# One search's order, homes, banks and engines for a two-branch kernel, replaced by another's

## The chip, the cores and the metric

The kernel runs on one core of a Trainium2 chip. The metric is the device time of one execution in microseconds; the median of three runs of the kernel before is 277.72 us (277.55 to 278.22).

## The reference

Two independent branches are computed over 2048 positions and set side by side in a bf16 output of 896 columns.

```python
# branch A: linear attention, 16 heads of 28, x is 2048 x 448
q, k, v = heads of (x @ wqkv)
phi(t) = concat[softmax(t @ w_phi), softmax(-(t @ w_phi))]     # per head, 56 features
kv = phi(k)^T @ v;  z = sum over positions of phi(k)
a = ((phi(q) @ kv) / (phi(q) @ z + 1e-6)) @ wo                   # 2048 x 448

# branch B: state-space convolution, 448 channels, 256 complex states
dt = exp(log_dt);  A = A_re + 1j*A_im
K[d, l] = Re sum_n C[d,n] * exp(dt*A*l)[d,n] * dt*B[d,n]         # l = 0..2047
y = causal convolution of u with K (rfft, product, irfft) + u * Dskip
out = concat([a, y], axis=-1)                                    # 2048 x 896
```

## The kernel before

Every instruction group is first recorded and only then issued. Helpers (`tt`, `act`, `copy`, `mms`, `dma`, `turn`, `total`) add 1366 units to a `Plan`; a unit is one instruction, or one group of matmuls into one PSUM tile. `Plan.run` then walks a string, `ORDER`, whose tokens are a unit's number and a letter for the engine that issues it: P for TensorE (PE), A for ScalarE (ACT), D for VectorE (DVE), G for GpSimd (POOL), S for SyncE (SP). Each engine executes its own units in the order of the string. A letter can be chosen where a helper allows it: `copy` (L342, an eviction from PSUM) is a cast on ACT or on DVE; `total` (L379 or L381, a sum in place) is a DVE add or an accumulating DMA that POOL issues; `dma` (L366) is issued by SP, POOL or ACT.

All of SBUF is one tile of 212,800 bytes a partition. `HOMES` gives each buffer its byte address, and buffers whose lives do not overlap share bytes. `BANKS` gives each PSUM tile one of eight banks. So a unit waits for its operands and for the readers of whatever lay in its home or bank before.

Branch A has sixteen key tiles (`key_tile`: exponentials on ACT, reciprocals L801 and products on DVE, sums over positions on PE), then four query groups (`query`, q0 to q3): exponentials, reciprocals L844 and L847, evictions, a product, a sum, a transpose by DMA (`turn`, L371, SP), the product with `wo`, an eviction and a store.

Branch B transforms u (`signal_spectrum`) and builds K in eight chunks of 56 channels, k = 0 to 7. Each chunk runs through the same cycle:

- `dampings` and `rotations` (rot k): PE makes phases, and ACT applies Exp and Sin to them. Exp and Sin need different tables, so ACT loads a table at each turn (L332 ACT_TABLE_LOAD, 17 in all, before and after).
- `damp` (damp k): POOL sets one row (L731, zero k); DVE multiplies tables `W[k]` and `E[k]` with L322. It needs rot k.
- `hi_tables` (hi k): products on DVE and five sums by `total`, each feeding the next.
- `build_k` (build k.1, then build k.0): 112 matmuls each, both reading `W[k]`; an eviction of each, 128x343.

All eight `W[k]` lie over each other, so rot k+1 on ACT must wait until build k on PE has read `W[k]`. In groups of two chunks follow 36 small DMAs that scatter K into place (`scatter_k`, sc0 to sc3; SP and POOL share them), `kernel_spectrum` (ks), the products `conv_group` (conv g.0 and g.1, DVE, with sums by `total`) and `inverse` (inv, matmuls, evictions, stores).

A part of the early chain of powers of H (`powers`) also uses `total`: units 90, 93, 96 and 99 on POOL, whose result DVE needs for the next doubling.

Of the kernel before, what the change touches and what calls it, by code (L numbers as in the profile page):

```python
# [91 lines left out]
0S 2A 3A 4S 5S 7S 28G 43P 44A 45D 42D 6S 46P 52A 49A 47P 30G 53D 71P 54A 72A 55D 73P 38G 51A 74A 50A 8S 140G 75P 77D  # L92
37S 48A 80D 76P 79D 17S 78D 57A 82D 56A 58D 81D 59D 649P 654A 61A 25S 657A 60A 655A 646P 648A 656A 39S 62D 650A 139G
141S 40S 69A 64A 142G 651A 143D 63D 144D 653A 95D 652A 88D 94D 89D 189S 190G 639P 19S 636P 65A 22S 41G 68A 191D 151P
647A 168P 640A 21S 18S 642A 638A 20S 118P 119A 225P 645A 226A 145P 637A 70D 169A 112P 192D 104D 210P 66D 23S 644A 24S
126P 643A 127A 641A 216P 211A 186P 102A 676D 113A 96G 180P 90G 219P 67D 92D 187A 217A 207P 114P 146A 218G 91D 97D 115A
93G 100A 122P 123A 213P 159P 98D 152A 214A 208A 103D 107A 680D 12S 124P 156P 116P 199P 234P 117A 200A 125A 34G 120P
675D 101D 235A 682D 677D 181A 121A 10S 9S 678D 681D 248P 105A 270P 272A 109D 259P 99G 660D 273A 262A 659D 171P 679D
201P 13S 220A 221G 250A 202A 195P 236G 196A 661D 174P 11S 170S 108D 261A 110A 172A 175A 106D 147P 212G 292P 294A 157A
303P 160A 295A 158G 183P 184A 658S 663D 662D 281P 283A 111D 237P 240A 14S 711D 148A 710D 712G 35G 203S 29G 165P 306A  # L100
664D 284A 166A 209G 239A 305A 149P 251A 204P 336P 150A 338A 153P 193P 188S 205A 194A 690P 154A 339A 665D 215G 666D
667D 669D 668D 670D 672D 671D 176S 696A 709S 714D 197P 687P 691A 155S 700P 673D 713D 688A 715D 27S 716D 693A 717D 198A
718D 297S 674G 685P 683P 689A 692A 695A 719D 694A 720D 708A 701A 707A 731D 721D 26S 1S 703A 161G 697P 698A 727D 699A
31G 725G 705A 173S 704A 314P 83P 722D 228P 206S 723D 684A 84A 129S 724G 686A 177P 702A 726D 229A 178A 179G 706A 85A
325P 730D 222P 733D 231P 223A 728D 833P 298P 842S 317A 227S 729D 732D 87A 264S 736P 328A 844D 843D 1025D 232A 167G
845D 327A 734P 893G 894D 15S 846D 316A 839A 330S 835A 837A 847D 86A 737A 841A 838A 836A 299D 265P 848D 830P 832A 735D
849D 895D 850D 834A 275S 266D 851D 331P 332D 896G 831A 840A 757G 820P 823P 16S 829A 825A 853D 852D 863D 822A 326P 854D
856D 827A 329A 855D 828A 758G 859D 861D 860D 824A 162P 826A 821A 163A 380P 383A 382A 369P 371A 372A 864D 862D 865D
286S 224S 866D 358P 402P 897D 898D 899D 751S 304P 900D 752S 901D 884P 902D 391P 360A 253S 361A 394A 393A 871P 742S
857G 333D 404A 769G 858G 182G 872A 754S 308S 405A 32G 307A 867P 868A 869P 890A 870D 276P 277D 886A 341S 342P 230S 396S  # L110
343D 888A 891A 887A 892A 885A 903D 904D 1026D 889A 770S 363S 164G 881P 874P 385S 905D 765G 883A 882A 1027D 748S 906D
# [5 lines left out]
355D 337P 1018A 1022A 320P 740G 321D 340A 366D 285A 763S 311D 1012P 1013A 260P 322D 1014A 425P 1039G 293P 1020A 1045D
263A 296A 1041D 759S 1017A 1042D 422P 1048D 953S 741S 749S 1021A 1019A 249P 252A 1043D 939S 936S 419P 1044D 421A 427A
951S 1047D 420A 476P 943G 424A 478A 428P 430A 289D 950G 744S 482P 376D 935G 944S 233G 344D 1051P 429A 484A 477A 1049P
929G 750G 760G 1066P 743S 1075S 426A 1052A 483A 423A 1073A 1207D 955S 245D 1063P 1072A 1065A 246P 256D 410D 957G 257P  # L120
267D 247P 258P 269P 947G 1074A 1050A 1070A 268P 279P 377D 300D 280P 291P 302P 290P 301P 312P 1076D 323P 313P 324P
1071A 1064A 335P 334P 345P 356P 773S 346P 357P 1068A 1067A 925S 473P 937S 924S 766S 771G 368P 367P 745S 378P 753G
1056P 1208D 379P 390P 1069A 401P 412P 946S 1077D 1078D 1080D 1061A 1206G 952G 1079D 1081D 1083D 932S 389P 1082D 1053P
400P 411P 949S 474A 1209G 1211D 930S 1084D 475A 1210D 775S 1055A 417D 1085D 416D 1062A 1057A 1054A 755S 780S 1058A
1060A 756S 768S 414D 533P 535A 418D 534A 479P 1086D 413D 931S 415D 1087D 530P 1096D 1088D 138G 954G 928G 772G 767G
431P 1089D 1093D 927G 776P 777A 1059A 785S 786P 455P 456A 439P 440A 443P 1097D 461P 462A 536P 432D 1092D 1212G 790S
778P 444A 481A 433D 480A 781P 782A 779A 783P 130G 787A 457P 459P 1214D 460A 1213D 437P 438A 441P 788P 789A 442A 434D
537A 791P 792A 458A 956S 527P 532A 528A 941G 1099D 1187P 1193A 1190A 945G 435D 1094D 1095D 1098D 793P 794A 531A 529A
137S 784A 1090G 1091G 1100P 1101A 131S 942G 133G 1215G 436D 795D 1102P 922S 1189A 746S 1184P 1197P 1188A 923S 445D
134S 463D 538A 1191A 1103A 1216D 1192A 1185A 1186A 1217D 485P 635S 1200A 1198A 797G 961P 1218G 774D 515P 807D 962A  # L130
1194P 1196A 796D 806D 486D 1205A 1195A 1202A 1199A 799D 1204A 1201A 803P 808D 136S 1128S 487D 965P 446G 539P 1135S
938S 1125S 798D 800P 1105G 1126G 1203A 1222G 516A 963P 1112S 1139G 966A 511P 512A 809G 1259D 488D 1219D 1123S 1257G
1258D 1120S 959S 1220D 1221G 964A 1260G 1223D 1225D 1137G 811G 1134G 489D 1228D 495P 496A 509P 510A 969P 967P 970A
# [52 lines left out]
BANKS = "2246060577464565566424057205213025364344223317722252233000363614704367562041217134315736107506766202\  # L186
# [880 lines left out]
```

## Time and profile before

| What | Value |
|---|---|
| Median of three runs | 277.72 us (277.55 to 278.22) |
| Profiled execution, its own time | 275.77 us |
| Its span, first to last instruction | 274.0 us |
| Mean granted TensorE clock | 0.979 |
| PE, DVE, ACT, POOL busy | 85%, 90%, 86%, 36% of the span |

The profiled execution stands 0.7% under the median of the runs, so changes are added up against 275.77 and then carried over to the median. A busy share is an average over very different stretches. In the lists, a wait is the idle time of an engine just before an instruction, put down to what ended it. In a list of waits the three numbers are the total in us, the number of waits, and the longest one. In a grouped list `x68 | 71.8, 1083 | 4.2` means 68 instructions, 71.8 us busy, 1083 ns each on average, 4.2 us idle ahead of them. Matmuls overlap in the pipeline, so a mean per matmul is longer than their spacing.

### The profile page before, as it was taken

What the parts mean: (1) busy time and instruction counts of PE and PEld (TensorE: products, weight loads), DVE (VectorE), ACT (ScalarE), POOL (GpSimd) and SP (SyncE); (2) the same over time, 40 slices, a digit from 0 to 9 for tenths busy, and PEclk for the clock granted to TensorE, in tenths of its full rate; (3) what the DMA queues carried; (4) which work ended last, traced back from release to release, by engine and by line L of the source; (5) the groups of instructions that cost most, each with busy time, mean ns of one, the idle gap of its engine ahead of it and who ended that gap; (6) DMA issues with size and microseconds to landing.
All of it is one profiled execution on the core that took longest, in us unless ns stands there. A gap on an engine that the chain in (4) does not pass through costs nothing.

```text
span 274.0 us, 10764 instructions
## 1 busy us (share of the span) xinstructions
PE 233.8 (85%) x4620; PEld 199.8 (73%) x4620; DVE 247.1 (90%) x334; ACT 235.0 (86%) x414; POOL 97.3 (36%) x169
## 2 busy tenths in 40 slices
PE   3825788999896797698999998979997998998994
PEld 3724686789786476376669977979895998788964
DVE  1699989999999899799899999997999989999891
ACT  3999999999999998996998999998969992756551
POOL 2400221260113330302942362176757210657450
PEclk9995999999999999999999999998999999999998
DMA  7996996455548797981431699399987797125764
GB/s 188 327 362 119 173 208 118 140 153 129 130 110 126 130 165 115 122 93 22 63 75 19 198 237 203 52 250 164 142 135 105 187 219 138 11 16 93 177 178 113
DMA packets 66969, 39.10 MB, mean 143 GB/s; under 512 B 53372, under 2 KB 62954, under 8 KB 66666
## 3 DMA queue, kind: packets, MB, share of 16 engines
q1 hardware_dynamic: 57914, 23.22, 40.7%
q0 software_dynamic: 8400, 14.94, 28.5%
q8 instruction: 36, 0.59, 1.0%
q10 hardware_dynamic: 608, 0.26, 0.3%
q14 instruction: 11, 0.09, 0.1%
HBM read 13.18 MB, written 6.42 MB: 72 GB/s over the span
## 4 chain that ended last, share of the span: by engine, by line
PE 31%; ACT 30%; DVE 19%; issue 8%; DMA 6%; SPq 4%; POOL 0%; ACTq 0%; DVEq 0%; POOLq 0%
PE psum L351 31%; ACT sbuf L332 20%; DVE sbuf L322 16%; ACT sbuf L342 5%; DMA sbuf<-sbuf 4%; SPq L366 4%; ACT L332 4%; ACT sbuf L337 1%; DVE sbuf L379 1%; DMA sbuf<-in_B_A_re_dram 1%; DVE sbuf L326 1%; DVE sbuf L545 0%; POOL sbuf L381 0%; DVE sbuf L342 0%; DVE sbuf L801 0%
## 5 line engine op out<-in xcount | busy, mean ns | idle before, releaser
L351 PE MATMUL psum<-sbuf 128*128 128x112 bf16 (+7 forms) x4620 | 233.8, 247 | 36.4 <-ACT sbuf L332 15.8
L351 PEld LDWEIGHTS <-sbuf 128*128 128x128 bf16 (+4 forms) x4620 | 199.8, 117 | 70.2 <-issue 38.5
L322 DVE TENSOR_TENSOR sbuf<-sbuf 128x896 bf16<-128x896 bf16 (+6 forms) x232 | 191.6, 873 | 13.8 <-ACT sbuf L332 9.2
L332 ACT ACTIVATE sbuf<-psum 128x448 bf16<-128x448 f32 (+4 forms) x221 | 138.5, 759 | 2.4 <-PE psum L351 2.0
L342 ACT CAST sbuf<-psum 128x448 bf16<-128x448 f32 (+3 forms) x167 | 84.1, 591 | 25.5 <-PE psum L351 25.0
L366 POOL DMA_DIRECT2D sbuf<-sbuf x68 | 46.8, 821 | 37.8 <-ACT sbuf L342 22.6
L381 POOL DMA_DIRECT2D sbuf<-sbuf x25 | 24.2, 994 | 66.1 <-DVE sbuf L322 47.4
L379 DVE TENSOR_TENSOR sbuf<-sbuf 128x896 bf16<-128x896 bf16 (+1 forms) x43 | 35.4, 833 | 0.4
L332 ACT ACT_TABLE_LOAD x17 | 21.8, 1283 | 5.0 <-PE psum L351 3.1
L366 POOL DMA_DIRECT2D out_dram<-sbuf x17 | 11.2, 693 | 17.0 <-ACT sbuf L342 17.0
L366 POOL DMA_DIRECT2D SUd<-sbuf x13 | 8.2, 649 | 23.8 <-ACT sbuf L342 23.8
L322 DVE TENSOR_TENSOR sbuf<-psum,sbuf 128x896 f32<-128x896 f32 (+4 forms) x14 | 8.8, 654 | 5.1 <-ACT sbuf L332 3.8
L731 POOL MEMSET sbuf<- 128x112 bf16 x16 | 3.7, 328 | 10.6 <-PE psum L351 10.4
L801 DVE RECIPROCAL sbuf<-psum 128x32 bf16<-128x32 f32 x16 | 5.3, 342 | 0.2 <-PE psum L351 0.2
L337 ACT CAST sbuf<-sbuf 128x1792 bf16<-128x1792 f32 x3 | 5.4, 1788 | 0.0
L337 ACT CAST sbuf<-psum 128x896 bf16<-128x896 f32 x2 | 1.8, 909 | 2.8 <-PE psum L351 2.8
L326 DVE SCALAR_TENSOR_TENSOR sbuf<-sbuf 128x64 f32<-128x64 f32 (+2 forms) x7 | 4.1, 590 | 0.0
L844 DVE RECIPROCAL sbuf<-psum 128x128 f32<-128x128 f32 x4 | 3.8, 949 | 0.2 <-PE psum L351 0.2
L366 POOL DMA_DIRECT2D sbuf<-SUd x2 | 1.7, 826 | 6.3 <-DVE sbuf L322 6.3
L342 DVE CAST sbuf<-psum 128x448 bf16<-128x448 f32 (+1 forms) x5 | 2.9, 583 | 0.9 <-PE psum L351 0.9
L332 ACT ACTIVATE sbuf<-sbuf 128x1792 f32<-128x1792 f32 x2 | 3.5, 1757 | 0.0
L847 DVE RECIPROCAL sbuf<-sbuf 128x64 f32<-128x64 f32 x4 | 2.1, 535 | 1.4 <-DMA sbuf<-sbuf 1.4
(21 smaller groups left out, 18.6 us busy)
## 6 DMA issues: line engine op xcount, KB each, us to landing
sbuf<-sbuf POOLq DMA_DIRECT2D x20, 224.0 KB, 4.9
sbuf<-sbuf POOLq DMA_DIRECT2D x8, 448.0 KB, 6.0
sbuf<-const SPq DMA_DIRECT2D x4, 640.0 KB
sbuf<-const SPq DMA_DIRECT2D x2, 1024.0 KB
out_dram<-sbuf POOLq DMA_DIRECT2D x17, 112.0 KB, 3.0
sbuf<-SUd SPq DMA_DIRECT2D x4, 448.0 KB
out_dram<-sbuf SPq DMA_DIRECT2D x15, 112.0 KB
SUd<-sbuf POOLq DMA_DIRECT2D x13, 112.0 KB, 2.7
```

The costliest lines, as they stand in the source:

```text
L322: lambda e: nc.vector.tensor_tensor(out=at(out_), in0=at(a), in1=at(b), op=op), [whose(a), whose(b)], [out_])
L326: lambda e: nc.vector.scalar_tensor_tensor(out=at(out_), in0=at(a), scalar=sc, in1=at(b), op0=op0, op1=op1),
L332: lambda e: nc.scalar.activation(at(out_), at(a), func, scale=scale, bias=bias), [whose(a)], [out_],
L337: plan.add({"ACT": 0.039 + sbuf + count(out_) * 0.8333e-3}, lambda e: nc.scalar.copy(at(out_), at(a)), [whose(a)], [out_])
L342: lambda e: (nc.scalar.copy if e == "ACT" else nc.vector.tensor_copy)(at(out_), at(a)), [whose(a)], [out_])
L351: nc.tensor.matmul(out_, lhsT=lhsT, rhs=rhs, start=start, stop=stop, **kw)
L366: plan.add({e: own[e] for e in engs}, lambda e: QUEUES[e].dma_start(out=out_, in_=in_, **kw), r, w, load=pieces / 16000 * max(11, 7.5 + 0. ...
L379: nc.vector.tensor_tensor(out=dst, in0=dst, in1=t2, op=ALU.add)
L381: nc.gpsimd.dma_start(out=view(dst), in_=view(t2), accum_op=ALU.add, max_dma_last_dim=3584)
L731: pool(0.5, lambda en: [nc.gpsimd.memset(w[:, c, ZERO, :], float(np.sqrt(0.5))) for c in range(2)], [], [w[:, 0, ZERO, :], w[:, 1, ZERO, :]])
L801: nc.vector.reciprocal(rk, pz.t)
L844: plan.add({"DVE": 0.868}, lambda e: nc.vector.reciprocal(rz[:, :, :, :], at(ndv(1))), [pz], [rz[:, :, :, :]])
```

## The change

The recorded units are the same, with the same instructions in each. `ORDER`, `HOMES` and `BANKS` are replaced as a whole. A few lines of the difference show the kind:

```diff
 ORDER = """
...
-392P 395A 1030D 242S 349A 1002P 1006A 1003A 909G 315P 318A 365D 920P 921A 1008A 1032D 918P 1011A 1031D 1033D 33G 1007A
-271P 919A 926G 399D 1009A 739S 274A 934G 761S 128S 403P 1035D 1034D 1004A 1036D 319S 185S 406A 352S 747S 287P 288D
...
-958D 1284P 1285A 1156A 1159D 1282P 1283A 1289S 1288S 1300S 1308G 1150A 470P 1315S 1293G 1146A 1310S 1309G 525A 1291S
...
+1031D 352S 1033D 1035D 920P 921A 918P 1034D 1036D 320P 1011A 1006A 919D 762G 276P 277D 321D 954G 1008A 1007A 271P 353P
...
+1324G 1155P 471A 1153P 589A 1156A 987G 816G 572D 617P 1142G 991D 519S 1273G 1284P 1285D 577S 573S 993G 472G 1282P
...
-         "K0": [88576], "t2h": [181472], "s2": [69728, 195808], "held": [109952], "W": [119328, 110624, 116256,
-         118048, 118048, 118048, 113440, 113440], "E": [9056, 149504, 109984, 202080, 202080, 171072, 194304, 171008],
...
+         [35008], "t2h": [191584], "s2": [111648, 94432], "held": [98464], "W": [118816, 112160, 118816, 117536,
+         117536, 117760, 116416, 116416], "E": [174208, 174208, 173344, 174208, 206208, 139840, 54528, 194848], "U":
...
-BANKS = "2246060577464565566424057205213025364344223317722252233000363614704367562041217134315736107506766202\
+BANKS = "7640202565721731031727014073070016571136546750056015233240173003466121051167540541120273055062300601\
...
```

Units that change their engine:

| From, to | Units |
|---|---|
| Eviction, ACT to DVE | 919 (build3.0) and 1285 (build7.1), 128x343; 815, 263, 351, 384, 575, 611, 618, 128x448; 86, 128x112 |
| Eviction, DVE to ACT | 870 (build2.1), 128x343; 471 (q0.3) and 615 (q3.1), 128x448 |
| Sum, DVE to POOL | 808, 1030, 1263, 1266, 128x1792; 464, 845, 905, 993, 128x896 |
| Sum, POOL to DVE | 500, 811, 979, 1218, 1260, 128x896 |
| DMA issues | SP has 15 fewer, POOL 16 more of L366 and 3 more of L381; among them the 1 MB table G2 (const6) and two F tiles (const1) move to POOL; the scatters go from 24, 20, 17 and 18 of 36 on SP to 18, 18, 20 and 18 |

On ACT, the number of instructions ahead of its 8th, 10th, 14th and 17th table load is 159, 197, 282 and 327 before and 155, 193, 277 and 324 after. On PE, 18 matmuls of ks1.0.0 and 4 of q1.3 stand last ahead of the phases of rot6.0 before; 18 of ks1.2.0, 18 of ks1.0.0 and 32 of inv0.0 do after, and the last of these need DVE's products of conv0.0. In the last group, 18 scatters on SP are followed by five transposes on SP in both; PE's order from there to the end is the same. On POOL, 96G stands earlier among its units than before and 90G later, and the DVE units that wait for them are in another order. The second of the four L847 on DVE waits before for a POOL-issued DMA that reads the bytes of its home; after, it waits for none, and the third L844 waits for eleven DMA queues, those of scatters that read the bytes of its home. The homes of `W[k]` still lie over each other, and so the cycle rot, damp, build, rot stands.

Three places in the order follow. The first is DVE behind damp3, whose last two products are 128x2688 (L322). Before:

```order
L322 TENSOR_TENSOR sbuf<-sbuf 128x16x112 x2
L322 TENSOR_TENSOR sbuf<-sbuf 128x2688 x2
L322 TENSOR_TENSOR sbuf<-sbuf 128x1792
L322 TENSOR_TENSOR sbuf<-sbuf 128x2x448
L379 TENSOR_TENSOR sbuf<-sbuf 128x1792
L801 RECIPROCAL sbuf<-psum 128x2x16
L322 TENSOR_TENSOR sbuf<-sbuf 128x1792 x2
L379 TENSOR_TENSOR sbuf<-sbuf 128x1792
L322 TENSOR_TENSOR sbuf<-sbuf 128x2x448
L322 TENSOR_TENSOR sbuf<-sbuf 128x896 x2
L379 TENSOR_TENSOR sbuf<-sbuf 128x896
```

After (the CAST is the eviction of build3.0, unit 919):

```order
L322 TENSOR_TENSOR sbuf<-sbuf 128x2688 x2
L322 TENSOR_TENSOR sbuf<-sbuf 128x2x448
L322 TENSOR_TENSOR sbuf<-sbuf 128x1792 x2
L379 TENSOR_TENSOR sbuf<-sbuf 128x1792
L322 TENSOR_TENSOR sbuf<-sbuf 128x896 x2
L379 TENSOR_TENSOR sbuf<-sbuf 128x896
L342 CAST sbuf<-psum 128x49x7
L801 RECIPROCAL sbuf<-psum 128x2x16 x2
L322 TENSOR_TENSOR sbuf<-sbuf 128x2x448
L322 TENSOR_TENSOR sbuf<-sbuf 128x896 x2
L322 TENSOR_TENSOR sbuf<-sbuf 128x2x448
```

An eviction that ACT made now stands among DVE's products, behind seven instructions since damp3 (896 elements in 2x448, two of 1792 and a sum of 1792, two of 896 and a sum of 896); the second sum of 1792 is POOL's now.

The second is ACT from its 14th table load on, where the Sin work of rot6 begins; 128x896 is a unit of rot6.0. Before:

```order
L332 ACT_TABLE_LOAD
L332 ACTIVATE sbuf<-psum 128x448
L332 ACTIVATE sbuf<-psum 128x896
L342 CAST sbuf<-psum 128x2x224
L332 ACTIVATE sbuf<-psum 128x2x448
L332 ACTIVATE sbuf<-psum 128x4x112
L332 ACTIVATE sbuf<-psum 128x2x448
L332 ACTIVATE sbuf<-psum 128x448
L332 ACTIVATE sbuf<-psum 128x896
```

After:

```order
L332 ACT_TABLE_LOAD
L332 ACTIVATE sbuf<-psum 128x448
L332 ACTIVATE sbuf<-psum 128x4x112 x2
L342 CAST sbuf<-psum 128x2x224
L332 ACTIVATE sbuf<-psum 128x896
L342 CAST sbuf<-psum 128x448 x2
L332 ACTIVATE sbuf<-psum 128x2x448
L332 ACTIVATE sbuf<-psum 128x448
L332 ACTIVATE sbuf<-psum 128x2x448
L332 ACTIVATE sbuf<-psum 128x896
```

The first unit of rot6.0 moved from the second place behind the table load to the fifth, and two more evictions stand in the stretch.

The third is POOL's queue around the sum of conv0.0, unit 797. Before, it is the first of the two L381 of 128x896 in one row:

```order
L381 DMA sbuf<-sbuf 128x896
L731 MEMSET sbuf 128x112 x2
L366 DMA sbuf<-sbuf 128x1x28
L366 DMA sbuf<-in_A_wo_dram 32x1x448
L381 DMA sbuf<-sbuf 128x1792
L381 DMA sbuf<-sbuf 128x896 x2
L381 DMA sbuf<-sbuf 128x2x448
L366 DMA sbuf<-sbuf 128x1x28
L366 DMA sbuf<-sbuf 72x1x28
```

After, it is the L381 of 128x896, and the transfer of 128x4096 is G2:

```order
L366 DMA sbuf<-const 128x4096
L366 DMA sbuf<-sbuf 4x1x28
L366 DMA sbuf<-const 128x512
L381 DMA sbuf<-sbuf 128x1792
L366 DMA sbuf<-sbuf 72x1x28
L381 DMA sbuf<-sbuf 128x896
L366 DMA sbuf<-in_A_wo_dram 16x1x448
L381 DMA sbuf<-sbuf 128x2x448 x2
```

G2, a load of a late constant and more scatters moved ahead of the sum of conv0.0 and of the sum of 1792 in hi6 before it; a second sum of a query (2x448) now follows.

More of the change, by code (lines that the diff above doesn't have):

```diff
@@ L97 @@
[L97 to L111, printed above, removed]
@@ L117 @@
[L117 to L121, printed above, removed]
@@ L152 @@
-1180G 557A 616S 472G 1359D 1347A 558S 1348S 1360P 1363P 612S 1364A 1361D 1362S 1365S
-"""
-HOMES = {"PID": [62432], "H": [155776], "AT": [50432], "TH": [38592], "PW128": [42176], "PW256": [56704], "PW512":
-         [98720], "P64": [104608], "ident": [8384], "negid": [104096], "ones": [99168], "LT": [87552], "half":
-         [108576], "HZ": [34304], "IDX": [205600], "xT": [177376, 141792, 34944, 94848], "WpQ": [19072], "WpK":
[3 rows of a table removed]
-         "rawCre": [164352], "rawCim": [166528], "rawBre": [87680], "rawBim": [196576], "ldt": [141280], "dt":
[11 rows of a table removed]
-         12736, 99168, 50368, 173056], "EKT": [148640, 171200, 47552, 86176, 173056, 104352, 49536, 166528, 55808,
[3 rows of a table removed]
-         [22656, 99168, 177280, 56832, 34944, 170112, 70432, 82272], "oT_": [191680, 55808, 54784, 193280, 53760,
[9 rows of a table removed]
```

106 lines of the change are left out of this document (67 added, 39 removed), and 48 rows, old and new, of the table HOMES.

## Prediction

> **What bounds the kernel now.** I read busy shares first, then the chain of work that ended last, then each engine's waits. Busy time per engine and the chain's shares:
>
> ```profile
> PE 233.8 (85%) x4620; PEld 199.8 (73%) x4620; DVE 247.1 (90%) x334; ACT 235.0 (86%) x414; POOL 97.3 (36%) x169
> PE 31%; ACT 30%; DVE 19%; issue 8%; DMA 6%; SPq 4%; POOL 0%; ACTq 0%; DVEq 0%; POOLq 0%
> ```
>
> Three engines are nearly full and the chain changes between them, so no engine alone sets the time. DVE, the fullest, is the best account book: whatever goes wrong elsewhere shows as DVE idle time. Its waits (us in total, times, longest):
>
> ```profile
> DVE sbuf L322 <- ACT sbuf L332: 13.0, 11, 3.8
> ...
> DVE sbuf L847 <- DMA sbuf<-sbuf: 1.4, 1, 1.4
> DVE sbuf L322 <- DMA sbuf<-sbuf: 1.3, 1, 1.3
> ```
>
> Two of the eleven waits on ACT lie in the opening work, as their shapes show in the grouped list (the last numbers are idle time):
>
> ```profile
> L322 DVE TENSOR_TENSOR sbuf<-psum,sbuf 128x896 bf16<-128x896 f32 x2 | 2.1, 1086 | 3.8 <-ACT sbuf L332 3.8
> L322 DVE TENSOR_TENSOR sbuf<-sbuf 112x448 bf16<-112x448 bf16 x1 | 0.6, 626 | 3.2 <-ACT sbuf L332 3.2
> ```
>
> That leaves 13.0 - 3.8 - 3.2 = 6.0 us in nine waits, and these are damps waiting for their rotations. The timeline of DVE (start, us, instruction, idle before) shows the largest late ones, and two waits on DMAs:
>
> ```profile
> 36.45 1.09 DVE L322 TENSOR_TENSOR sbuf<-sbuf 128x1792 bf16<-128x1792 bf16 x1 [1.31 <-DMA sbuf<-sbuf]
> 132.73 0.39 DVE L322 TENSOR_TENSOR sbuf<-sbuf 128x448 bf16<-128x448 bf16 x1 [0.85 <-ACT sbuf L332]
> 188.29 1.09 DVE L322 TENSOR_TENSOR sbuf<-sbuf 128x1792 bf16<-128x1792 bf16 x1 [0.69 <-ACT sbuf L332]
> 192.02 0.55 DVE L847 RECIPROCAL sbuf<-sbuf 128x64 f32<-128x64 f32 x1 [1.39 <-DMA sbuf<-sbuf]
> 220.21 6.42 DVE L322 TENSOR_TENSOR sbuf<-sbuf 128x1792 bf16<-128x1792 bf16 x6 [0.99 <-ACT sbuf L332]
> ```
>
> So the middle is a cycle: ACT rotates, DVE damps, PE builds, and only then may ACT rotate the next chunk, since all `W` share bytes. Wherever ACT comes late DVE stops. The end has another limit, the chain's last part:
>
> ```profile
> 227.22 4.73 PE psum L351 x152
> ...
> 234.39 0.97 ACT sbuf L342 x2
> 235.41 0.70 SPq L366
> ...
> 246.66 0.70 SPq L366
> 247.40 3.49 DMA sbuf<-sbuf
> ...
> 266.67 3.53 PE psum L351 x68
> 270.27 0.53 ACT sbuf L342
> ```
>
> From build7 (227.22) to the end of the span at 274.0 it runs build, 16 scatters one by one on SP, spectrum, convolution, inverse: 46.8 us, released by damp7. So the time is, near enough, the moment of damp7 plus 46.8 us.
>
> **The change, part by part.** I sum on DVE's account, whose rows follow, against the profiled execution's 275.77 us (span 274.0), which lies 0.7% under the median of the runs, 277.72.
>
> ```profile
> L379 DVE TENSOR_TENSOR sbuf<-sbuf 128x1792 bf16<-128x1792 bf16 x20 | 21.5, 1080 | 0.3
> L379 DVE TENSOR_TENSOR sbuf<-sbuf 128x896 bf16<-128x896 bf16 x23 | 14.2, 619 | 0.2
> L342 DVE CAST sbuf<-psum 128x448 bf16<-128x448 f32 x3 | 1.9, 620 | 0.9 <-PE psum L351 0.9
> L342 DVE CAST sbuf<-psum 128x343 bf16<-128x343 f32 x2 | 1.1, 528 | 0.0
> L342 ACT CAST sbuf<-psum 128x448 bf16<-128x448 f32 x147 | 75.0, 599 | 16.4 <-PE psum L351 15.9
> L322 DVE TENSOR_TENSOR sbuf<-sbuf 128x1792 bf16<-128x1792 bf16 x68 | 71.8, 1083 | 4.2 <-ACT sbuf L332 2.0 <-DMA sbuf<-sbuf 1.3 <-ACT sbuf L342 0.3
> L322 DVE TENSOR_TENSOR sbuf<-sbuf 128x896 bf16<-128x896 bf16 x88 | 50.6, 612 | 0.4
> ```
>
> *DVE's work.* Out go four sums of 1792 and four of 896: 4 x 1.080 + 4 x 0.619 = 6.80 us. In come five sums of 896, 3.10 us. Evictions: seven of 128x448 in and two out, 5 x 0.620 = 3.10; two of 128x343 in and one out, 0.53; one of 128x112, which no DVE row shows: from the two cast rows, 105 columns cost 92 ns, so about 0.33. Net -6.80 + 3.10 + 3.10 + 0.53 + 0.33 = **+0.3 us**. DVE gets no lighter: sums were swapped for evictions.
>
> *ACT's lead.* The same swap takes work off ACT: three, four or five instructions fewer stand ahead of its 8th, 10th, 14th and 17th table load. At 0.60 us each (the 448 row) ACT reaches those points 1.8 to 3.0 us sooner, if nothing else holds it. I take the last, the 17th, ahead of rot7 and so of damp7: 3 x 0.60 = **-1.8 us**, out of the 6.0 us of damp waits. Bounds: 0, if ACT merely waits longer for build k to free `W`; -3.0, five instructions. I stand nearer the middle because ACT's chain share, 30%, is as large as PE's.
>
> *build3.0's eviction and the reciprocals behind it on DVE.* This is the first place of the order. Now DVE must wait for both builds:
>
> ```profile
> 121.02 3.58 PE psum L351 x137
> 124.59 0.42 issue
> 125.02 2.36 PE psum L351 x75
> 127.40 0.54 ACT sbuf L342
> ```
>
> PE took 3.58 + 0.42 + 2.36 = 6.36 us. The cover on DVE is one product as 2x448 (0.612), two of 1792 (2.17), a sum (1.08), two of 896 (1.22) and a sum (0.62): 5.70 us. So **+0.7 us**; behind the wait are key reciprocals, whose sums PE waits for. Bounds 0 (the build starts before the last damp product retires) and +1.5 (0.7 plus the next damp's 0.85 wait at 132.73 repeated by it). The other moved evictions of queries and keys have PE done long before in the order; nothing added.
>
> *The powers.* At 36.45 DVE waited 1.31 us for an accumulating DMA. 96G comes earlier, 90G later, with consumers reordered: **0**, bounds -1.3 (the wait gone) and +1.0 (one more issue ahead, 0.994 us, the L381 row below).
>
> *rot6.0.* On PE its phases now stand behind 18 + 32 - 4 = 46 more matmuls; at 3.53 us for 68 (the chain's row at 266.67) that is 2.4 us. ACT in turn arrives up to 3.0 us sooner, but took rot6.0 straight from PE. damp6 waited 0.69 us already (188.29). Bounds: -0.7 (that wait goes) and +1.7 (2.4 less the 0.7 held already); I take the middle, **+0.5**, since neither row is nearer.
>
> *The reciprocal L847 of a query.* It waited 1.39 us for a DMA that still read the bytes of its home; at the new home no DMA stands among its waits. **-1.4**, for the row shows DVE doing nothing else. Bounds: -1.4; on the other side DVE's next damp may take the freed time as its own wait, since the chain passes here on PE, and the third L844 now waits for eleven DMA queues, the scatters that read its home. I take those as long landed; if not, the nearest row is again 1.39, so +1.4.
>
> *POOL and SP.*
>
> ```profile
> L366 POOL DMA_DIRECT2D sbuf<-sbuf x68 | 46.8, 821 | 37.8 <-ACT sbuf L342 22.6 <-PE psum L351 9.5 <-DVE sbuf L326 2.9
> L381 POOL DMA_DIRECT2D sbuf<-sbuf x25 | 24.2, 994 | 66.1 <-DVE sbuf L322 47.4
> sbuf<-sbuf POOLq DMA_DIRECT2D x8, 448.0 KB, 6.0
> 135.00:160.00 25.00, 24.23 (x456) 20.05 (x455) 24.58 (x38) 23.99 (x41) 11.01 (x19) 1.00 0.44 112
> 160.00:181.00 21.00, 20.29 (x481) 18.11 (x479) 20.47 (x29) 20.69 (x43) 8.23 (x12) 1.00 0.76 180
> ```
>
> POOL issues 16 more DMAs and three more sums: 16 x 0.82 + 3 x 0.99 = 16.1 us on an engine that is 64% idle. In the two stretches ahead of conv0.0's sum it was busy 11.01 + 8.23 of 46 us, so even all of it fits. A sum of 448 KB on POOL lands 6.0 us after its issue (the median row above), where DVE needs 1.1; the moved ones (hi2, hi3, hi4, hi7, conv, q) have other DVE work ahead of their readers in the order. **0**, covered by that work; without it, one costs up to 6.0 - 1.1 = 4.9 us. An issue on POOL took 0.82 us, on SP in the tail 0.70; if that 0.12 were contention with DVE and DVE paid as much, 19 issues would add 2.3 us. No row shows DVE paying: its 896 products and sums took 612 and 619 ns. Bounds 0 and +2.3.
>
> *A rule against this.* The Trainium skill (SBUF — State Buffer, "Who interferes with whom") says that a DVE instruction with two SBUF inputs competes with GpSimd instructions that read SBUF, and that copies and casts on DVE may take the shared ports and block descriptor writing. By that rule the moved issues and the added casts hinder each other, and the sum with the 2.3 us just named would be +0.6 us in place of -1.7. The trace neither proves it nor excludes it, since no row here shows POOL issuing beside an idle DVE.
>
> *The tail.* SP has 18 scatters there before and after, PE the same order: **0**, bounds one scatter less or more, -0.7 and +0.7.
>
> Sum: 0.3 - 1.8 + 0.7 + 0 + 0.5 - 1.4 + 0 + 0 = -1.7 us, so 275.77 - 1.7 = 274.1 us profiled, and 277.72 - 1.7 = **276.0 us** for the median. All lower bounds together give -6.8 (270.9), all upper ones +8.9 (286.6).
>
> **Rivals.** Two rows of the chain, one window and one row of PE's timeline bear on them:
>
> ```profile
> 136.92 11.92 PE psum L351 x247
> 148.91 0.11 ACT L332
> 184.00:187.00 3.00, 3.00 (x34) 3.00 (x35) 2.96 (x8) 1.98 (x4) 0.71 (x1) 0.50 0.89 159
> 183.92 2.33 PE L351 MATMUL psum<-sbuf 128*128 128x112 bf16 x23 [1.67 <-issue]
> ```
>
> *No change.* One `W` buffer still ties rot, damp and build. If ACT was late because build k freed `W` late, ACT's lead only lengthens its own wait, and the reciprocal's gap returns at the next damp: 0.3 + 0.7 + 0.5 - 1.4 = +0.1, so 277.8. POOL's issues paid by DVE, +2.3 on the forecast, end in the same place: 278.3. For the first: PE is on the chain for 11.92 us right ahead of a table load. Against it: the damp waits end on ACT's rotations, and ACT is 30% of the chain.
>
> *Slower: rot6.0 behind inv0.0.* inv0.0 needs DVE's last product of conv0.0, and PE takes its queue in order, so rot6.0 now waits for DVE, and DVE's damp6 for rot6.0. The 2.4 us of matmuls can run at half clock: in the row from 184 (PEclk is the third value from the right) PE at 184 to 187 got 0.50 after 1.67 us idle, so 2.4 becomes 4.8. Less the 0.7 held already that is +4.1, and ACT's lead is gone with it: 0.3 + 0.7 + 4.1 - 1.4 = +3.7, or, with half of the 4.1 covered by other DVE work, +1.65: about 279.4. It decides from about 2.2 us of added wait at damp6 (0.3 + 0.7 + 2.2 - 1.4 = 1.8, less a lead of 1.0 still gained, is the 0.8 that can be told). The clock rule of the Trainium skill (TensorE: Matmul & The Clock Gate, Part 1) asks for an idle window of some 3.4 us; the trace differs, with half clock after a shorter gap; by the rule the 2.4 us stay 2.4, and this case would be 1.2 us nearer to no change.
>
> *Slower: POOL's landings.* G2 (1 MB) and scatters now stand ahead of conv0.0's sum on POOL. If POOL falls behind by one landing there, a reader on DVE waits 4.9 us less what DVE can put between (three products of 1792, 3.2 us): 1.7, and ACT's lead is lost to it as well: 0.1 + 1.7 = +1.8, 279.5. For it: POOL's share of the hi sums of 1792 grows by three; against it: the 64% idle.
>
> **How the numbers follow.** About 0.3% (0.83 us) can be told from no change. Forecast, 0.45, with 274.5 to 276.9 of its own; a larger gain (the powers' wait and ACT's full 3.0 us too, -1.7 - 1.3 - 1.2 = -4.2, so 273.5), 0.05; no change, 0.2, of which 0.05 for contention; rot6.0, 0.2; POOL's landings, 0.1. Faster 0.5, same 0.2, slower 0.3. The range holds all these cases, leaves out the corners where several bounds fall together, and adds 0.7 below the larger gain and 0.5 above the slowest: 272.8 to 280.0.
>
> **What would show it.** DVE's busy time stays within 0.5 us of 247.1; its waits on ACT's L332 fall from 13.0 to about 11; the L847 wait is gone; a DVE cast after damp3 waits 0.7 us for PE; build7 starts near 225.5, with 46.8 us behind it. It is wrong if DVE's waits on DMAs grow past 2.7 us, if a new wait for PE stands ahead of damp6, or if the part behind build7 changes by over 1 us.

## The result and the profile after

The changed kernel is slower: 281.95 us against 277.22 us, medians of 20 runs each; the ratio of times is 1.010, with a 95% interval of 1.005 to 1.015. Six more runs gave a median of 286.34 us (ratio 1.017, 1.008 to 1.026). The forecast was 276.0. Runs of the changed kernel scatter from 276 to 288 us; the ratios leave out disturbed, longer ones, the medians hold them all, and both profiles of this very kernel (283.55 us, span 281.6, and 285.69 us) are of longer ones, so that what is claimed of the ratio rests on its variants.

The page's busy times and the chain's shares in the profile of 283.55 us:

```profile
PE 237.6 (84%) x4620; PEld 202.6 (72%) x4620; DVE 247.5 (88%) x338; ACT 232.8 (83%) x407; POOL 109.1 (39%) x188
...
PE 34%; ACT 18%; DVE 11%; issue 6%; DMA 2%; POOL 0%; ACTq 0%; DVEq 0%
```

DVE works as long as before (247.5 against 247.1) and ACT a little less (232.8 against 235.0), so the work moved as forecast. The chain's shares say less: here they add up to some 71% of the span, since the chain could be followed back only to 77 us; from 80 us on ACT has 25% of the time, and 29% before. The time is in DVE's idle stretches. Its list of waits, and below it the row of before that one of them is to be compared with:

```profile
DVE sbuf L322 <- ACT sbuf L332: 7.5, 8, 3.4
DVE sbuf L342 <- PE psum L351: 4.0, 4, 2.2
DVE sbuf L322 <- DMA sbuf<-in_B_u_dram,sbuf: 3.1, 1, 3.1
DVE sbuf L342 <- ACT sbuf L342: 3.1, 2, 2.4
DVE sbuf L466 <- DMA sbuf<-const: 2.5, 1, 2.5
DVE sbuf L322 <- issue: 2.3, 3, 1.9
DVE sbuf L801 <- PE psum L351: 2.2, 2, 1.2
```

```profile
DVE sbuf L342 <- PE psum L351: 0.9, 1, 0.9
```

DVE's waits on ACT's L332 fell from 13.0 to 7.5, less than the 11 I expected. But 3.4 and 0.4 us of the 7.5 lie in the opening work, as 7.0 of the 13.0 did, and one opening wait only changed its name (L466 waits 2.5 us for a DMA where a product waited 3.2 us for ACT). The damps' own waits fell from 6.0 to 3.7. L847 no longer waits, and no wait for a sum of H16 is listed. New are the third row and most of the waits ahead of evictions (L342). DVE's timeline shows the opening waits, the third row, and the eviction of build3.0 at its new place:

```profile
3.05 0.63 DVE L322 TENSOR_TENSOR sbuf<-sbuf 112x448 bf16<-112x448 bf16 x1 [0.38 <-ACT sbuf L332]
7.06 1.09 DVE L322 TENSOR_TENSOR sbuf<-psum,sbuf 128x896 bf16<-128x896 f32 x1 [3.38 <-ACT sbuf L332]
...
25.08 3.10 DVE L322 TENSOR_TENSOR sbuf<-sbuf 128x1792 bf16<-128x1792 bf16 x3 [3.07 <-DMA sbuf<-in_B_u_dram,sbuf]
...
133.90 0.54 DVE L342 CAST sbuf<-psum 128x343 bf16<-128x343 f32 x1 [0.74 <-PE psum L351]
...
191.78 0.53 DVE L847 RECIPROCAL sbuf<-sbuf 128x64 f32<-128x64 f32 x1
```

At 25.08 stands ab0, the first product of u (unit 144). It waits for the gather of u, an indirect DMA that POOL issues (L647). PE waits behind it, since its order now has two transforms of u ahead of exps0, as PE's timeline shows; and near the end PE has two holes that no wait explains:

```profile
26.32 5.86 PE L351 MATMUL psum<-sbuf 128*128 128x112 bf16 x72 [9.40 <-DVE sbuf L322]
...
235.20 3.48 PE L351 MATMUL psum<-sbuf 128*32 128x49 bf16 x128 [2.19 <-issue]
240.57 1.62 PE L351 MATMUL psum<-sbuf 112*128 112x8 bf16 x44 [1.90 <-issue]
```

The row at 235.20 is the rest of build7, with which the part begins that sets the end. So two suspects were there from the start: the head, before 36 us, and the tail. Two of the prediction's signs of being wrong had come: DVE waited 5.6 us for DMAs, not 2.7 at most, and from build7 to the end it took 51.25 us, not 46.8. And build7 began at 230.40, not near 225.5.

### The profile page after: what moved, and what is told of

It is laid out like the page before. It is cut to its first block, busy times and chain, and to the rows that moved or that the text cites. A ratio compares the mean times of both kernels' runs of the same rounds, so it can differ in the third digit from the quotient of the medians.

```text
span 281.6 us, 10785 instructions
## 1 busy us (share of the span) xinstructions
PE 237.6 (84%) x4620; PEld 202.6 (72%) x4620; DVE 247.5 (88%) x338; ACT 232.8 (83%) x407; POOL 109.1 (39%) x188
## 3 DMA queue, kind: packets, MB, share of 16 engines
HBM read 13.18 MB, written 6.42 MB: 70 GB/s over the span
## 4 chain that ended last, share of the span: by engine, by line
PE 34%; ACT 18%; DVE 11%; issue 6%; DMA 2%; POOL 0%; ACTq 0%; DVEq 0%
PE psum L351 34%; ACT sbuf L332 14%; DVE sbuf L322 9%; ACT sbuf L342 4%; DMA sbuf<-sbuf 2%; ACT L332 1%; DVE sbuf L379 1%; DVE sbuf L342 1%; DVE sbuf L801 0%; POOL sbuf L381 0%; ACTq L332 0%; DVEq L322 0%; DVEq L801 0%; ACTq L342 0%
## 5 line engine op out<-in xcount | busy, mean ns | idle before, releaser
L351 PE MATMUL psum<-sbuf 128*32 128x49 bf16 (+8 forms) x4620 | 237.6, 248 | 40.2 <-DVE sbuf L322 11.0
L351 PEld LDWEIGHTS <-sbuf 128*128 128x128 bf16 (+4 forms) x4620 | 202.6, 118 | 75.1 <-issue 42.7
L322 DVE TENSOR_TENSOR sbuf<-sbuf 128x1792 bf16<-128x1792 bf16 (+8 forms) x232 | 191.1, 874 | 10.8 <-ACT sbuf L332 4.1
L332 ACT ACTIVATE sbuf<-psum 128x448 bf16<-128x448 f32 (+4 forms) x221 | 137.3, 756 | 6.2 <-PE psum L351 5.8
L342 ACT CAST sbuf<-psum 128x448 bf16<-128x448 f32 (+3 forms) x160 | 80.5, 597 | 31.8 <-PE psum L351 31.4
L366 POOL DMA_DIRECT2D sbuf<-sbuf x75 | 52.6, 811 | 33.8 <-ACT sbuf L332 10.6
L381 POOL DMA_DIRECT2D sbuf<-sbuf x28 | 26.4, 960 | 99.9 <-DVE sbuf L322 66.8
L379 DVE TENSOR_TENSOR sbuf<-sbuf 128x896 bf16<-128x896 bf16 (+1 forms) x40 | 32.1, 808 | 0.5
L366 POOL DMA_DIRECT2D out_dram<-sbuf x19 | 13.6, 750 | 16.9 <-ACT sbuf L342 15.2
L322 DVE TENSOR_TENSOR sbuf<-psum,sbuf 128x896 f32<-128x896 f32 (+4 forms) x14 | 8.9, 658 | 5.8 <-ACT sbuf L332 3.4
L342 DVE CAST sbuf<-psum 128x448 bf16<-128x448 f32 (+2 forms) x12 | 6.8, 571 | 7.1 <-PE psum L351 4.0
L366 POOL DMA_DIRECT2D SUd<-sbuf x14 | 9.5, 710 | 3.4 <-ACT sbuf L342 3.4
L844 DVE RECIPROCAL sbuf<-psum 128x128 f32<-128x128 f32 x4 | 3.8, 950 | 0.3 <-PE psum L351 0.3
L366 POOL DMA_DIRECT2D sbuf<-in_A_wo_dram x4 | 2.7, 664 | 3.4 <-PE psum L351 3.1
L366 POOL DMA_DIRECT2D sbuf<-SUd x4 | 3.6, 903 | 0.0
```

The costliest lines, as they stand in the source:

```text
L322: lambda e: nc.vector.tensor_tensor(out=at(out_), in0=at(a), in1=at(b), op=op), [whose(a), whose(b)], [out_])
L332: lambda e: nc.scalar.activation(at(out_), at(a), func, scale=scale, bias=bias), [whose(a)], [out_],
L342: lambda e: (nc.scalar.copy if e == "ACT" else nc.vector.tensor_copy)(at(out_), at(a)), [whose(a)], [out_])
L351: nc.tensor.matmul(out_, lhsT=lhsT, rhs=rhs, start=start, stop=stop, **kw)
L366: plan.add({e: own[e] for e in engs}, lambda e: QUEUES[e].dma_start(out=out_, in_=in_, **kw), r, w, load=pieces / 16000 * max(11, 7.5 + 0. ...
L379: nc.vector.tensor_tensor(out=dst, in0=dst, in1=t2, op=ALU.add)
```

## The experiments

All times are medians, with the ratio to the kernel before in runs on the same chip. In the list of what ran beside what, "u loads" are `load_su`: four DMAs of 448 KB that bring the parked transforms of u back for groups 2 (1141, 1142) and 3 (1323, 1324). In the kernel before their homes came free early: 1323 and 1324 were issued at 210 us, 1142 and 1141 at 217.5 and 223.2. In the new homes none can run before the products of conv1.1 have read what lies there; three run at 220 to 223 us on POOL, ahead of build7, and 1323 at 249 us between the last scatters.

**The kernel again.**

> The changed kernel as it is, for a second measurement and a second profile. Theory A (the loss lies in the tail: the loads of the parked signal spectra, load_su, now run at 220 to 250 us and collide with PE's instruction loads and with the last scatters): again 1% to 1.5% slower than before, build7 to the end about 4 us longer than the 46.8 us of before, and a hole on PE of 1 to 2 us in build7. Theory B (the loss lies in the head: DVE waits 3.07 us for the gather of u before ab0): slower by the same, but the wait of about 3 us at ab0 is there and build7 to the end is within 1 us of before. Theory C (only a chance half clock of TensorE in the profiled run): neither wait returns, and the time is within 0.5% of before.

Measured 286.34 us, ratio 1.017 (1.008 to 1.026). The row of ab0 on DVE's timeline:

```profile
27.70 3.10 DVE L322 TENSOR_TENSOR sbuf<-sbuf 128x1792 bf16<-128x1792 bf16 x3 [5.62 <-DMA sbuf<-in_B_u_dram,sbuf]
```

The gather's wait is 5.62 us this time, 3.07 before: a landing that moves from run to run. Theory C, chance alone, is out as a cause of the ratio. But Theory A's two signs are missing from this profile. PE runs through build7 (236.97 to 242.60) without a hole, and from build7 to the end it takes 46.81 us, against 46.77 before:

```profile
222.33 34.95 PE L351 MATMUL psum<-sbuf 128*128 128x112 bf16 x682 [0.64 <-ACT sbuf L332]
```

So the hole in build7 comes and goes in one and the same kernel, and the price of the tail must come from the times of variants.

**u loads of group 3, one or both, behind the last scatter.** One load, then both:

```diff
 ... 1301S 1292S
-1323G (among the scatters)   -1324G (221 us)
+1323S                        +1324S (second kernel only)
```

> One load of su3 (448 KB, unit 1323) is issued on SP behind the last scatter of group 3 in place of on POOL among the scatters. Theory A: the last scatter that ks3.0 needs lands about 3.5 us after its issue and not 5.5, so 1.5 to 2 us faster than the changed kernel, unless conv3.0 then waits for the load (about 7 us from its issue, 9 us of time for it). Theory B and C: no change, within 0.3% of the changed kernel.

> Both loads of su3 (2 x 448 KB) are issued on SP behind the last scatter, so that only two loads of 448 KB are left at 220 to 224 us. Theory A: PE's hole in build7 (2.2 us) shrinks below 1 us, the half clock behind it goes, and the scatters land sooner: 3 to 4.5 us faster than the changed kernel, level with before; at risk, conv3.0 waits up to 2 us for the loads. Theory B and C: within 0.5% of the changed kernel.

One: 279.32 us, ratio 1.007 (1.001 to 1.012), a step that can't be told from none. Both: 277.50 us, ratio 1.004 (1.000 to 1.009). By these figures Theory A accounts for more than half of the loss in the ratio (1.010 to 1.004, or 1.6 us, where 3 to 4.5 were expected), though the two intervals overlap; the median falls by 4.4 us. In the profile with both moved PE has no hole in build7, and it takes 45.65 us from there to the end.

**The same fault put into the kernel before.**

```diff
-1324S -1141S -1323G (210 to 223 us)
+1142G 1324G 1141G (216 us)   +1311G 1323G (among the scatters)
```

> The kernel before with the four half loads of su2 and su3 placed about as in the changed kernel: three of them together on POOL at 217 to 221 us, the fourth on POOL among the last scatters. Theory A: the scatters land later and PE's instructions too, 1.5 to 3 us slower than the kernel before. If the tail differs for another reason (order of the scatters, the eviction on DVE): within 0.5 us.

Measured 279.50 us, ratio 1.013 (1.007 to 1.019): a loss of this kind appears in the other kernel, with its own homes, banks and engines, and by more than was expected. This is the stronger half of the evidence. The chain of that profile goes through PE, with holes of 2.43 and 1.76 us in build7, and 50.72 us from build7 to the end:

```profile
225.36 1.64 PE psum L351 x44
227.00 2.43 issue
229.43 3.33 PE psum L351 x117
232.76 1.76 issue
234.53 8.22 PE psum L351 x98
```

**ab0 moved behind three products on DVE.**

```diff
-69A 144D 650A ... 95D 59D 96G
+69A 650A ... 95D 59D 144D 96G
```

> On DVE one product (ab0, unit 144) moves behind three others that don't need the gather, so that 2.3 of the 3.07 us of waiting for the gather is filled with work. Theory B: 1.5 to 2.3 us faster than the changed kernel. Theory A and C: the lead is lost at a later damp, which waits for ACT or PE: within 0.3% of the changed kernel.

Measured 280.99 us, ratio 1.013 (1.009 to 1.017): nothing gained. Its timeline shows two reasons:

```profile
26.50 1.09 DVE L322 TENSOR_TENSOR sbuf<-sbuf 128x1792 bf16<-128x1792 bf16 x1 [2.67 <-DMA sbuf<-in_B_u_dram,sbuf]
28.83 9.28 DVE L322 TENSOR_TENSOR sbuf<-sbuf 128x1792 bf16<-128x1792 bf16 x8 [1.23 <-DMA sbuf<-in_B_u_dram,sbuf]
```

ab0 still waits 2.67 us, since the gather landed at 26.5 us and not at 25.1, and the next product (ab1) waits for the second gather in turn. This one move didn't cover the wait; the gather itself must come sooner.

**G earlier on SP; A_re back on ACT.** Two guesses at what delays the gather, each alone:

```diff
-8S ... 141S 37S 38S 189S 18S 25S        (G, unit 25, behind u and a transpose)
+8S ... 25S 141S 37S 38S 189S 18S
```
```diff
-0S 2A 3S
+0S 2A 3A
```

> In the changed kernel the 1 MB table G is issued on SP ahead of the two loads of u and of the transposes, as in the kernel before, in place of behind them. Theory H (the first products of u, ab0, wait for the gather, whose packets now share the DMA engines with G and with a transpose): G is through before the gather begins, the gather lands at 21 to 22 us and not at 23 to 30, the wait of 3 to 5.6 us at ab0 falls below 1 us, and the time falls by 2 to 4 us, to 278 to 280. Theory I (the gather is late because it is issued late, or by chance): the wait at ab0 and the time stay, 281 to 283.

> In the changed kernel the first raw load (A_re) goes back from SP to ACT's queue, so that SP's six other raw loads come 0.4 us sooner, and the gather on POOL, which is held back until they are in, is issued up to 0.9 us sooner. Theory I: the gather lands 1 us or more sooner and the time falls by 1 to 2 us. Theory H: G and the transpose still share the engines with the gather; within 1 us of the changed kernel (282).

G early: 284.69 us, ratio 1.027 (1.020 to 1.034), no faster than the changed kernel (1.010 and 1.017); ab0 waited 6.93 us in its profile:

```profile
28.49 3.09 DVE L322 TENSOR_TENSOR sbuf<-sbuf 128x1792 bf16<-128x1792 bf16 x3 [6.93 <-DMA sbuf<-in_B_u_dram,sbuf]
```

Theory H is out as far as G goes. A_re on ACT: 279.87 us, ratio 1.012 (1.008 to 1.015). The ratio is that of the changed kernel; the median is 2.1 us below it. The wait at ab0 is gone from the timeline, and another has come, at H64:

```profile
37.34 6.10 DVE L322 TENSOR_TENSOR sbuf<-sbuf 128x1792 bf16<-128x1792 bf16 x6 [2.67 <-DMA sbuf<-sbuf]
```

So the place of A_re's load matters for the wait, and not for the ratio: with it on ACT's queue ab0 waits in none of six profiles, with it on SP in five of six (not in the one with both u loads moved). The reason that Theory I gave, a gather issued sooner, doesn't hold: issued at 9.57 us in the kernel with G early, it landed at 28.47; issued at 9.65 in a kernel with A_re on ACT (the one below with evictions back), it landed at 19.65. What slows it isn't settled; the reverse test doesn't show it either.

```diff
-17S ... 25S ... 141S 40S 189S 190G 19S
+17S ... 141S 40S 189S 190G 19S 25S      (kernel before)
```

> The kernel before with G issued on SP behind the two loads of u and the second transpose, about as in the changed kernel. Theory H: the gather's packets are held up as in the changed kernel, a wait of 1 to 4 us appears at ab0, and the time rises by 1 to 3 us, to 277 to 279, with a wider spread of runs. Theory I: within 0.5 us of the kernel before.

Measured 276.77 us, ratio 1.003 (1.000 to 1.007): no difference that can be told, and in its profile the wait is not at ab0 but at H64, 6.81 us.

**Repairs together.** First all three, then without G's:

> Three repairs of the changed kernel together: G early, A_re on ACT, and both loads of su3 behind the last scatter. Theory A with H: head and tail are both mended, 274.5 to 276.5 us, level with the kernel before (276.0) or up to 0.5% faster. If sums, evictions and order of the middle cost something of their own: 277 to 279.

> The changed kernel with A_re's load back on ACT (gather 0.9 us sooner) and both loads of su3 behind the last scatter; G stays where the change put it. Theory A with I (tail: the loads of su3; head: the gather's time against the transposes): 275 to 277 us, with few runs above 280. If G's early place was what helped in the three repairs together, this one is 2 us slower than they were, 279 to 280.

With G early 277.44 us, ratio 1.005 (1.001 to 1.010); without it 276.69 us, ratio 1.005 (1.001 to 1.009). That is the second case of the first expectation: something in the middle costs time of its own. Against A_re alone (1.012) the u loads are worth 0.7%, or 1.8 us. PE's timeline, first with the loads ahead of build7 (A_re alone), then with the two of group 3 moved:

```profile
232.78 3.44 PE L351 MATMUL psum<-sbuf 128*32 128x49 bf16 x128 [0.96 <-issue]
236.51 3.66 PE L351 MATMUL psum<-sbuf 112*128 112x8 bf16 x65 [0.29 <-issue]
...
252.10 6.11 PE L351 MATMUL psum<-sbuf 128*128 128x112 bf16 x121 [1.00 <-DMA sbuf<-sbuf]
```

```profile
221.90 20.30 PE L351 MATMUL psum<-sbuf 128*128 128x112 bf16 x454 [0.57 <-ACT sbuf L342]
```

PE runs through build7 without a hole in the second, and the wait at 252.10, for the last scatters to land, is gone as well. That wait is the steadier sign: it was 1.0 to 1.3 us in four of the five profiles with all four loads in the changed places (all but the first), and 0.4 us at most in the six with two of them moved; in the kernel before it is 1.1 us. The window from 228 to 232 us shows what was there at that time; the DMA share is the last value but one. In order: the kernel before; the kernel before with late u loads; A_re alone; A_re with the u loads moved.

```profile
228.00:232.00 4.00, 3.95 (x166) 3.72 (x155) 3.97 (x10) 0.94 (x2) 0.00 (x0) 1.00 0.65 105
```
```profile
228.00:232.00 4.00, 2.57 (x108) 2.57 (x111) 1.40 (x4) 0.94 (x2) 0.00 (x0) 1.00 1.28 134
```
```profile
228.00:232.00 4.00, 3.83 (x124) 3.51 (x121) 3.83 (x8) 1.79 (x4) 0.00 (x0) 1.00 1.24 262
```
```profile
228.00:232.00 4.00, 4.00 (x117) 3.91 (x118) 3.87 (x7) 3.10 (x7) 0.00 (x0) 1.00 0.46 113
```

The DMA engines are overbooked (1.24 and 1.28) in the two kernels with u loads ahead of build7. But the kernel before has a hole as well, just behind its window:

```profile
232.78 17.16 PE L351 MATMUL psum<-sbuf 128*32 128x49 bf16 x278 [0.83 <-issue]
```

Over the whole of build7, from its first matmul to its last, eight of the sixteen profiles have holes, with a mean DMA share of 0.62 to 1.28, and eight have none, with 0.35 to 0.57. Among the eight without are three of the changed kernel with its loads in place (the second profile, ab0 moved, G early), where build7 began when the loads had all but landed; among those with holes are two that have the loads moved. So the holes go with busy DMA engines during build7, and the u loads are one way to make them busy, not the only one.

**Evictions back on ACT; sums back on their old engines.** Both on the repaired kernel:

```diff
-86D 919D 1285D
+86A 919A 1285A
```
```diff
-808G 845G 905G 993G 1030G 1263G 1266G 464G   500D 811D 979D 1218D 1260D
+808D 845D 905D 993D 1030D 1263D 1266D 464D   500G 811G 979G 1218G 1260G
```

> The same, and three of the ten evictions that the change moved to DVE go back to ACT: 86 (k0), 919 (build3.0) and 1285 (build7.1), which in the profiles of the changed kernel make DVE wait 0.7, 0.5 to 0.7 and 0 to 2.2 us for PE. Theory M (these waits on DVE are on the path): 1 to 1.5 us faster than the same kernel without it. Theory N (ACT hands over later by the same, so it is even): within 0.5 us.

> The kernel with the two repairs (A_re, su3), and all 13 sums whose engine the change swapped go back: eight from POOL to DVE (6.8 us of DVE's time), five from DVE to POOL (3.1 us). By the prediction's account of DVE's work: 3.7 us slower, at least 2. If DVE's work in the middle is covered by waits for ACT and PE: within 0.7 us. If the sums' landing on POOL had become a wait: 1 to 2 us faster.

Evictions back: 279.06 us, ratio 1.015 (1.008 to 1.021), some 1% or 2.6 us slower. Both theories are wrong: the moves are worth more than even. DVE's timeline after damp3 shows one reason: the wait for PE is not gone, it passes to the reciprocals (1.02 us), and then DVE waits for ACT, which now has the eviction:

```profile
132.59 0.57 DVE L801 RECIPROCAL sbuf<-psum 128x32 bf16<-128x32 f32 x2 [1.02 <-PE psum L351]
...
135.97 0.62 DVE L322 TENSOR_TENSOR sbuf<-sbuf 128x896 bf16<-128x896 bf16 x1 [1.27 <-ACT sbuf L342]
```

Sums back: 284.50 us, ratio 1.018 (1.010 to 1.026). The median rises by 7.8 us, the ratio by 1.3% or 3.5 us, which is about DVE's 3.7 us of added work. Five sums on POOL also bring a landing to wait for, 4.08 us for one of hi6:

```profile
196.32 4.13 DVE L322 TENSOR_TENSOR sbuf<-sbuf 128x896 bf16<-128x896 bf16 x5 [4.08 <-DMA sbuf<-sbuf]
```

**The sum of H16 on DVE.** In the repaired kernel H64 (unit 92) still waits for the sum that POOL issues for unit 90:

```profile
38.92 6.10 DVE L322 TENSOR_TENSOR sbuf<-sbuf 128x1792 bf16<-128x1792 bf16 x6 [3.94 <-DMA sbuf<-sbuf]
```

```diff
-90G
+90D
```

> The repaired kernel (A_re on ACT, su3 behind the scatters) with one sum of H16 (unit 90, 128x1792) on DVE and not on POOL. Theory P (the rest of the loss is that sum's landing): the wait of 3.9 us at H64 goes, 1.08 us of DVE's work comes in, and the time falls by 1 to 2.5 us, to 274.5 to 275.5, below the kernel before. Theory Q (the wait only covers work that is late anyway, at ACT or PE): within 0.5 us of 276.7.

> The kernel before with the same sum on DVE. Its profile shows 1.31 us at H64 for it (6.8 us in a profile of its variant with G late). Theory P: the median falls by 0 to 0.5 us and the runs above 279 go, since the long waits are there. Theory Q: DVE's 1.08 us more are added or hidden, median +0 to +1, and the spread stays.

Repaired kernel: 275.24 us, ratio 0.996 (0.992 to 0.999). Kernel before: 275.03 us, ratio 0.996 (0.992 to 1.000), against 276.91 us beside it. Theory P holds, in the kernel before by more than was expected. DVE's timeline of the repaired kernel has no idle time at that place any more (the row holds H64's products):

```profile
35.40 7.10 DVE L322 TENSOR_TENSOR sbuf<-sbuf 128x1792 bf16<-128x1792 bf16 x7
```

The repaired kernel with this sum on DVE beats both kernels, by 0.4% the one before; but so does the kernel before with the one letter changed.

## Why the prediction was wrong

*The first step that failed is the path behind ACT's lead: "the time is, near enough, the moment of damp7 plus 46.8 us".* The lead itself came, but it was lost again before build7. These are the moments (us) that tell it, out of six profiles; damp7's first product is the one that waits for rot7:

| Kernel | PE begins build0 | damp7's first product | damp7's last product ends | PE begins build7 | End |
|---|---|---|---|---|---|
| Before | 64.4 | 220.2 | 226.6 | 227.2 | 274.0 |
| Changed, first profile | 66.8 | 220.4 | 229.4 | 230.4 | 281.6 |
| A_re on ACT | 65.8 | 219.3 | 228.3 | 229.2 | 277.2 |
| A_re and u loads | 66.4 | 220.6 | 229.6 | 230.5 | 276.1 |
| The same, sum of H16 on DVE | 64.4 | 218.0 | 227.0 | 228.0 | 274.3 |
| Before, sum of H16 on DVE | 64.2 | 219.3 | 225.7 | 226.3 | 271.7 |

From build0 to damp7's first product it is 155.9 us before and 153.6 in the first profile after (154.3 to 156.6 and 153.0 to 154.5 in all profiles of the two kernels and their variants, 156.7 with the sums put back). That is about the lead that I summed, though not where I sought it: ACT's 17th table load itself came at 217.35, not 1.8 us ahead of 212.92. But build7 needs all eight products of damp7. Before, four of them, and two products and the sum of hi7.4, stand ahead of the wait for ACT; in the new order these seven stand behind it. DVE's timeline from that wait to the last product, where the row of before, in the prediction, has 6.42 us:

```profile
220.40 4.20 DVE L322 TENSOR_TENSOR sbuf<-sbuf 128x1792 bf16<-128x1792 bf16 x7 [1.01 <-ACT sbuf L332]
224.51 0.62 DVE L379 TENSOR_TENSOR sbuf<-sbuf 128x896 bf16<-128x896 bf16 x1
225.05 4.40 DVE L322 TENSOR_TENSOR sbuf<-sbuf 128x448 bf16<-128x448 bf16 x5
```

It is 9.04 us in every profile of the changed kernel and its variants (10.04 with the sums put back), and 6.42 in every one of the kernel before and its variants; to the start of build7 it is 9.9 to 10.6 us, against 7.0. So the sum lacks a term of +2.6 us (to the last product) to +3.0 (to build7, in the first profile), which takes the whole of the lead. The new order of these products was there to be read beforehand. No run put them back, so what this is worth in the time is read off the timelines, not shown by a change.

*The second is "the tail: 0, bounds -0.7 and +0.7".* I counted scatters on SP and the order of PE, and not the u loads, whose time is set by homes. Three experiments price it: 0.6% out of the changed kernel (1.010 to 1.004, with intervals that overlap), 0.7% out of the one with A_re mended (1.012 to 1.005), and 1.3% into the kernel before; that is 1.6 to 3.7 us. My rule that every step moved counts with its DMAs was not applied to `load_su`. With the forecast's -1.7, the +2.6 to +3.0 of damp7 and 1.6 to 1.8 of the u loads the sum would have been +2.5 to +3.1 us; the ratio of 1.010 is +2.8. That it fits is no proof of each term.

*The third is "the powers: 0, bounds -1.3 and +1.0".* The upper bound priced one issue on POOL, not a landing. The wait there moves from profile to profile: 0.3 to 6.8 us in those of the kernel before and its variants that keep this sum on POOL (1.31 in the first), none in the first profile after, 3.5 in the second, and 0.5 to 3.9 in the five with A_re on ACT. It is on the path: one sum on DVE gains 0.9% (1.005 to 0.996), and 0.4% in the kernel before; the difference of the two lies within the intervals, so how much of the 1.0% it explains is open. The nearest row for that bound was that wait's own, not a row on issues.

*The fourth is a term that I did not have: the first loads.* The sum began at 36 us. A raw load went from ACT to SP, and products and transforms of u came earlier on DVE and on PE; waits of 3.07, 5.62 and 6.93 us at ab0 followed. A_re alone doesn't lower the ratio, so this isn't shown to be part of the 1.0%. Single profiles show what such a wait does there (build0 began at 72.6 us in the second one, at 66.8 in the first); that it is why the medians differ by more than the ratio does (1.7%) is likely and not shown.

*Right by size:* DVE's work, +0.4 us for +0.3 forecast; build3.0's eviction, 0.74 us of waiting for +0.7 (in part luck: PE took 5.80 us and not 6.36, but began 0.37 us behind damp3's last product); L847's wait gone; the sums on POOL, whose 3.7 us are confirmed by the run that put them back. POOL's queue and its landings, the rival, did not become the bound except at H16, where the change had not moved the engine.

*ACT's lead* was right in its direction and its size up to damp7; the evictions put back cost 2.6 us, which fits it. At the end nothing is left of it: with A_re, the u loads and the sum of H16 mended the changed kernel stands at a ratio of 0.996, and the kernel before with that one sum on DVE does too. Besides damp7, DVE has new waits in the first profile: two reciprocals of keys (2.2 us), evictions that wait for PE and ACT (4.0 and 3.1 us in the list). I charged one moved eviction with a wait; the list shows six waits ahead of evictions. How much of that lies on the path is open.

*rot6.0* was a false alarm: no damp6 product waits in the profile after; +0.5 and the rival with 279.4 were both too dear, and the half clock of 184 to 187 us did not return there. The rule of the Trainium skill (SBUF — State Buffer, "Who interferes with whom") on the shared ports has left no sign in these runs, and was left out of the sum with reason: the swapped sums gained 3.5 us, and DVE's cast of 448 columns takes 611 to 620 ns as before.

## What to carry over

A sum of terms needs the path to its end: when a wait gets shorter, look up in the order how much the engine still has between that wait and the last product that the next engine needs. A table of homes moves transfers, though no instruction changes: for each large load, look up what its bytes held before, and when the last reader is through. Weigh a moved sum or load by its landing, and compare with the wait that stands in the trace. And where the cover of a wait is one product, look at what the product after it waits for. One profile isn't the kernel: a hole that one shows may be missing from the next.

## What the runs showed of the hardware

Most holes on PE that the profile calls "issue" end shortly after an instruction load. In the trace's DMA records the 36 loads of 16 KB on the instruction queue took 0.9 to 1.7 us in the profile after (median 1.1), but for one: that from 230.61 us took 3.19 us, and PE went on at 235.20, 1.39 us after its end. In the other holes PE goes on 1.2 to 1.5 us after such a load's end: 231.28 to 232.78 and 182.47 to 183.92 in the kernel before, 228.01 to 229.43 and 233.33 to 234.53 with late u loads, 239.28 to 240.57 after. In all sixteen profiles 49 of the 53 such holes of over 0.4 us end 1.2 to 1.8 us after the end of such a load. build7 has 224 short matmuls in under 6 us and so uses up instructions fast. In the first profile after, the last of three loads of 448 KB was under way until 233.08, and packets of under 512 bytes on the hardware queue took 0.93 of the DMA engines' time from 230.4 to 232.9 us. That the hole is the missing instructions is inferred from these times; no run took the load away alone. The Trainium skill (Runtime: NRT & Kernel Launch, "Instruction fetch mechanics") says that an engine fetches its instructions in blocks of 16 KB by a DMA queue of its own, and that the cost is mostly hidden. The trace agrees on the blocks; the cost was not hidden here, with holes in build7 of 0.54 to 2.43 us in eight of sixteen profiles.

A hole on PE can cost twice: behind the one of 2.19 us the granted clock was 0.50 from 236 to 239 us.

```profile
236.00:239.00 3.00, 2.68 (x104) 2.44 (x96) 2.97 (x4) 0.43 (x2) 0.00 (x0) 0.50 0.86 153
```

In the sixteen profiles there are 28 stretches at a clock of 0.50 between 40 and 262 us. Each lasts 3.41 us, and in the 3.41 us before each PE had been busy for 7% to 64%.
